# Pooled k by GpSimd sums and a DMA transpose, and tail u on array halves, in an attention and mixer kernel

## The chip, the cores and the metric

The kernel runs on one core of one Trainium2 chip. The metric is the device time of one execution in microseconds. The core has five engines with queues of their own, which run in order and meet through semaphores: PE (TensorE, matmuls), DVE (VectorE), ACT (ScalarE), POOL (GpSimd) and SP (SyncE, which here only issues DMAs). In this kernel PE writes to PSUM, DVE and ACT read PSUM and SBUF, and POOL works in SBUF and issues the loads, which also turn float32 into bf16. SP issues the output stores and the DMA transposes, which turn blocks of 128x128 bf16 in SBUF.

## What is computed

Batch 8, 8 heads, 576 rows, head size 64. First attention with pooled k and v (means over 8 rows, so 72 keys), then a mixer over rows ("token") and channels, with d_tok 256 and d_ch 1536:

```python
k_p = k.reshape(B, H, Sp, pool, D).mean(axis=3)      # pool = 8, Sp = 72
v_p = v.reshape(B, H, Sp, pool, D).mean(axis=3)
scores = scale * np.matmul(q, k_p.transpose(0, 1, 3, 2))
attn = softmax(scores)                                # over the 72 keys
x = heads_side_by_side(np.matmul(attn, v_p))          # (8, 576, 512)
h = np.maximum(x.transpose(0, 2, 1) @ w_tok1, 0.0) @ w_tok2
u = x + h.transpose(0, 2, 1)
out = u + np.maximum(u @ w_ch1, 0.0) @ w_ch2
```

## The kernel before, in words

**Tiles.** The 576 rows of a batch are 512 main rows and 64 tail rows. The main rows lie as 4 blocks of 128 rows (j = 0 to 3); the tail rows of two batches share one tile of 128 rows, one batch in partitions 0 to 63 and the other in 64 to 127. The pairs (`groups`) are (0, 7), (1, 2), (3, 4) and (5, 6); "slot" is a batch's place in its pair. PSUM tiles come from one ring of six (`pa`), so a PSUM tile that nobody has read yet can hold PE up.

**Stages of a batch.**
- *Pooled k*: `pool_k_sum` (L262) multiplies k by a pooling matrix, with k as the stationary operand: 32 matmuls for the main rows (L271) and 8 for the tail (L275), each with 64 output columns, on one half of the array or the other. The result lies transposed (head dimension in partitions) in two PSUM tiles. `pool_k_copy` (L279) casts it with two ACT and two DVE instructions (L284, L285) into `kbd`, a block-diagonal tile, two heads at a time. There are three `kbd` buffers.
- *Pooled v*: for batches 0 and 1 by matmuls (L292). From batch 2 on, v is loaded with 8 consecutive rows per partition (72 partitions, tile `vs`, two DMAs, L135), and `sum_v` (L296) adds the 8 rows on POOL, for two heads at a time, with three instructions (L302, L303, L304): twelve per batch. The sum goes to `vpx`.
- *Scores*: q is transposed on PE or by DMA (L553 for the main rows, L413 for tails). `Unit.do_S` makes the scores of half of the main rows on PE (L330), takes the maximum and subtracts it on DVE (L333, L335); `do_E` exponentiates on ACT (L343); `do_PT` transposes the probabilities, from batch 2 on with two DMAs on SP (L350). `TailUnit` does the same for tails, for both batches of a pair at once (L431, L437, L439, L446, L452); for pair (5, 6) it therefore needs `kbd` of 5 and of 6.
- *Values*: `values` (L394) multiplies probabilities and `vpx`; DVE divides by the sums (L398, L399). For tail pairs the two batches take the two halves of the array.
- *Token mix*: `do_AT` (L479, L483), then `do_u` (L513 for the blocks, L518 for a tail tile), each followed by a DVE addition of x (L515, L520). The tail's u is one accumulation of four matmuls with 128 output columns: the second matrix lies in two tiles `w2t`, padded with zeros, so that each batch adds to its own half of the rows. A tail's u is made with the pair's second batch, so after batches 2, 4, 6 and 7. `do_uT` transposes u by DMA on SP (L525).
- *Channel mix*: `channel_mix` makes GT (L776, ACT L778) and the output (L791, DVE L801), stored by SP (L829, L833). This is the bulk of PE's work.

**Order.** Each engine executes its instructions in the order in which the Python code emits them. For each batch b the channel mix of b is the main stream; the side stream holds the values and token mix of b + 1 (`value_stream`) and then the scores of b + 2 (`score_stream`). `weave` (L29) merges the two by costs written beside the items. The pooled k of batch b + 1 stands in the token mix of b (`mix_stream`, L580) if b + 1 opens a pair or belongs to the first two pairs; the pooled k of a pair's second batch stands in the score stream of the first (`own[1:]` in L701). Loads of batch b + 2 are issued by POOL in `load_gated` (L750): a tiny copy waits for the last transposed probabilities of batch b, then come the DMAs of k, q and v, then the twelve additions for v. Since POOL works in order, the next gate stands behind those additions.

Of the kernel before, what the change touches and what calls it, by code (L numbers as in the profile page):

```python
# [8 lines left out]
FP32 = mybir.dt.float32  # L9
BF16 = mybir.dt.bfloat16  # L10
# [38 lines left out]
def kernel(  # L49
# [56 lines left out]
    group_of = {b: g for g, members in enumerate(groups) for b in members}  # L106
    slot_of = {b: members.index(b) for members in groups for b in members}
    half = [slice(0, TAIL), slice(TAIL, P)]
    main_t, tail_t = {}, {}
    x_main, x_tail, u_main, uT_main, u_tail, uT_tail, ATs = {}, {}, {}, {}, {}, {}, {}  # L110

# [7 lines left out]
    def load(b, which=(0, 1, 2)):  # L119
        g = group_of[b]  # L120
        if b not in tail_t:
            tail_t[b] = [tail_pool.tile([P, H, D], BF16, name=n) for n in ("kt", "qt")]
            if b == 2:
                for t in tail_t[b]:
                    nc.gpsimd.memset(t[half[0]], 0.0)
            else:
                tail_t[groups[g][1]] = tail_t[b]
        main_t.setdefault(b, [None] * 3)
        for i in which:
            src = (k, q, v)[i]  # L130
            if i == 2 and b > 1:

                vs = v_pool.tile([P, H, POOL, D], BF16, name="vs")
                for r in (slice(0, SPM), slice(SPM, SP)):
                    nc.gpsimd.dma_start(out=vs[r].rearrange("p h t d -> p h (t d)"),  # L135
                                        in_=src[b].rearrange("h (p t) d -> p h (t d)", t=POOL)[r])
                main_t[b][i] = vs
                continue
            mt = (v_pool.tile([P, H, POOL, D], BF16, name="vs")[:, :, 0:NJ, :] if i == 2 else
                  kv_pool.tile([P, H, NJ, D], BF16, name=("km", "qm")[i]))  # L140
            main_t[b][i], tt = mt, tail_t[b][i]
            nc.gpsimd.dma_start(out=mt.rearrange("p h j d -> p h (j d)"),
                                in_=src[b, :, 0:MAIN, :].rearrange("h (p j) d -> p h (j d)", j=NJ))
# [52 lines left out]
    NB = 3  # L196
    kbd = [singles.tile([P, H, 2, SP], BF16, name=f"kbd{i}") for i in range(NB)]
    vpx = [singles.tile([SP, H, D + 1], BF16, name=f"vpx{i}") for i in range(NB)]
    for i in range(NB):
        eng = nc.vector if i == 0 else nc.any  # L200
        eng.memset(kbd[i], 0.0)
        eng.memset(vpx[i][:, :, D], float(POOL))

    NPB = 4
    prob_m = [singles.tile([P, 2, H, P], BF16, name=f"prob_m{i}") for i in range(NPB)]
    prob_t = [singles.tile([P, 2, HP, P], BF16, name=f"prob_t{i}") for i in range(2)]
# [14 lines left out]
    w1t = [singles.tile([P, DT], BF16, name=f"w1t{s}") for s in range(2)]  # L221
    w2r = gt_pool.tile([P, 2, S], BF16, name=f"GT{MAIN}")
    w2m = singles.tile([P, 2, NJ, P], BF16)
    w2t = [singles.tile([P, 2, P], BF16, name=f"w2t{s}") for s in range(2)]
    wc1 = singles.tile([P, 4, DC], BF16)
    wc2 = singles.tile([P, NM, DM], BF16)

    def load_w_tok():
        for s in range(2):
            nc.any.memset(w1t[s][half[1 - s]], 0.0)  # L230
            nc.any.memset(w2t[s][:, :, half[1 - s]], 0.0)
        nc.gpsimd.dma_start(out=w1m, in_=moe_w_tok1[0:MAIN, :].rearrange("(p j) n -> p j n", j=NJ))
        nc.gpsimd.dma_start(out=w1t[0][half[0], :], in_=moe_w_tok1[MAIN:S, :])
        nc.gpsimd.dma_start(out=w2r, in_=moe_w_tok2.rearrange("(c p) n -> p c n", p=P))
        nc.gpsimd.dma_start(out=w1t[1][half[1], :], in_=moe_w_tok1[MAIN:S, :])

    def split_w_tok2():
        for m in range(2):
            nc.gpsimd.tensor_copy(out=w2m[:, m], in_=w2r[:, m, 0:MAIN].rearrange("p (t j) -> p j t", j=NJ))
        for s in range(2):  # L240
            nc.gpsimd.tensor_copy(out=w2t[s][:, :, half[s]], in_=w2r[:, :, MAIN:S])

    def load_w_ch1():
        for i in range(3):
# [13 lines left out]

    def pool_k(b):
        pool_k_copy(b, pool_k_sum(b))  # L260

    def pool_k_sum(b):  # L262
        g, s = group_of[b], slot_of[b]
# [31 lines left out]

    def sum_v(b):  # L296

        vs, add = main_t[b][2][0:SP], ALU.add
        for h0 in range(0, H, 2):
            hs = slice(h0, h0 + 2)  # L300
            s4 = sum_pool.tile([P, 2, 4, D], FP32, name="s4")[0:SP]
            nc.gpsimd.tensor_tensor(out=s4, in0=vs[:, hs, 0:4], in1=vs[:, hs, 4:8], op=add)  # L302
            nc.gpsimd.tensor_tensor(out=s4[:, :, 0:2], in0=s4[:, :, 0:2], in1=s4[:, :, 2:4], op=add)  # L303
            nc.gpsimd.tensor_tensor(out=vpx[b % NB][:, hs, 0:D], in0=s4[:, :, 0], in1=s4[:, :, 1], op=add)  # L304

    class Unit:

# [31 lines left out]
        def do_E(self, i):  # L339
            h0, h1 = BANKS[i]  # L340
            if self.probs is None:
                self.probs = prob_m[(2 * self.b + self.jj) % NPB]
            nc.scalar.activation(out=self.probs[:, :, h0:h1, 0:SP].rearrange("p e h n -> p h e n"),  # L343
                                 in_=self.sh[i][:, 0:(h1 - h0) * 2].rearrange("p (h e) n -> p h e n", e=2),
                                 func=AF.Exp, scale=scale)

        def do_PT(self, e):
            self.pT[e] = pt_pool.tile([P, H, P], BF16, name="pT")
# [54 lines left out]
    class TailUnit:  # L403
# [39 lines left out]
        def do_E(self):  # L443
            self.probs = prob_t[self.g % 2]
            for i, sh in enumerate(self.sh):
                nc.scalar.activation(out=self.probs[:, i, :, 0:SP], in_=sh[:, 0:HP], func=AF.Exp, scale=scale)  # L446

        def do_PT(self):
            n = len(self.bs) * HP
# [16 lines left out]
    def token_mix(b):  # L466
# [40 lines left out]
                        acts(m, at_both[m])  # L507

        def do_u(j):
            u_ps = ps.tile([P, DM], FP32, name="pa")  # L510
            if j < NJ:
                for m in range(2):
                    nc.tensor.matmul(out=u_ps, lhsT=w2m[:, m, j, :], rhs=ATs[b][:, m, :],  # L513
                                     start=(m == 0), stop=(m == 1))
                nc.vector.tensor_tensor(out=u_main[b][:, j, :], in0=u_ps, in1=x_main[b][:, j, :], op=ALU.add)  # L515
            else:
                for i in range(4):
                    nc.tensor.matmul(out=u_ps, lhsT=w2t[i // 2][:, i % 2, :], rhs=ATs[groups[g][i // 2]][:, i % 2, :],  # L518
                                     start=(i == 0), stop=(i == 3))
                nc.vector.tensor_tensor(out=u_tail[g], in0=u_ps, in1=x_tail[g], op=ALU.add)  # L520

        def do_uT(j):
            us = u_main[b][:, j, :] if j < NJ else u_tail[g]
# [56 lines left out]
    def mix_stream(st, b, pooled=()):  # L580

        g, s = group_of[b], slot_of[b]
        add = adder(st)
        if b:
            u_main[b] = u_pool.tile([P, NJ, DM], BF16, name="um")
        uT_main[b] = u_pool.tile([P, 4, MAIN], BF16, name="uTm")
        if s == 1:
            u_tail[g] = ut_pool.tile([P, DM], BF16, name="ut")
            uT_tail[g] = ut_pool.tile([P, 4, P], BF16, name="uTt")
        do_AT, do_both_AT, do_u, do_uT, do_xT, do_uT0 = token_mix(b)  # L590
        if b == 0:
            return do_both_AT, do_xT, do_uT0
        add(1080, do_AT, 0)
        add(1080, do_AT, 1)
        for bb in pooled:
            add(KP, pool_k, bb)
        nj = NJ + s
        for j in range(nj + 1):
            if j < nj:
                add(690, do_u, j)  # L600
            if j >= 1:
                add(0, do_uT, j - 1)
# [98 lines left out]
    def score_stream(st, b):  # L701

        add = adder(st)
        a, c, t = parts[b]
        own = owned(b)
        if b == 3:
            add(KP, pool_k, b)
        add(SC, a.do_S, 0)
        add(SC, a.do_S, 1)
        add(0, a.do_E, 0)  # L710
        add(SC, a.do_S, 2)
        add(0, a.do_E, 1)
        add(0, a.do_E, 2)
        add(0, a.do_PT, 0)
        add(0, a.do_PT, 1)
        add(SC, c.do_S, 0)
        for bb in own[1:]:
            add(KP, pool_k, bb)
        add(SC, c.do_S, 1)
        add(0, c.do_E, 0)  # L720
        add(SC, c.do_S, 2)
        add(0, c.do_E, 1)
        add(0, c.do_E, 2)
        add(0, c.do_PT, 0)
        add(0, c.do_PT, 1)
        if t:
            add(2 * SC, t.do_S)
            add(0, t.do_E)
            add(0, t.do_PT)

    def value_stream(st, b):

# [17 lines left out]
    def load_gated(b, ready):  # L750

        nc.gpsimd.tensor_copy(out=gate, in_=ready())
        if b == 4:

            load(b - 1, (2,))
            load(b, (0, 2, 1))
            sum_v(b - 1)
        else:
            load(b, (0, 2, 1) if slot_of[b] else (0, 1, 2))
        sum_v(b)  # L760

    def channel_mix(uTs, us, dst, width, early=0):
# [90 lines left out]
               mybir.EngineType.SP, mybir.EngineType.Pool}  # L853
    with tc.manual_schedule(engines=engines):
        weave(Stream(), first_stream())
        for b in range(B):
            side = Stream()
            if b == 0:
                second_stream(side)
            elif b + 1 < B:  # L860
                value_stream(side, b + 1)
            if b + 2 < B:
                score_stream(side, b + 2)

            weave(c_stream(b), side, (2592.0, 3456.0)[b] if b <= 1 else 1728.0, 3456.0 if b == B - 2 else 1728.0)


# [28 lines left out]
```

## Time and profile before

| | us |
|---|---|
| runs: median of three (lowest, highest) | 282.71 (282.39, 283.29) |
| the profiled execution | 283.01 |
| its span, first to last instruction | 281.1 |
| PE busy | 270.1 |
| DVE, ACT, POOL busy | 161.1, 122.6, 104.4 |

The profile shows one execution. For each engine it counts the time in which instructions ran; matmuls overlap in the record, so a matmul's own duration (379 ns for 512 columns) is longer than its share of PE, and the distance from one start to the next is the better price. The granted TensorE clock is recorded as full (1.00) over the span, and the 16 DMA engines are busy at 90% or more in 20 consecutive of its 40 slices, from the second on. Times in the text are microseconds from the span's start. A row of the timeline gives start, duration, engine, line, operation, the tiles written and read, shape, and how many equal instructions were merged; in brackets stands idle time of the engine before it and what ended it. A row of the waits gives who waited for whom, the total, how often, and the longest.

### The profile page before, as it was taken

How to read it: one execution, taken by the hardware profiler on the slowest of the kernel's cores; microseconds unless marked ns; L12 is line 12 of the kernel's file. 1: busy time of each engine (PE TensorE's matmuls, PEld its weight loads, DVE VectorE, ACT ScalarE, POOL GpSimd, SP SyncE). 2: the span in 40 equal slices, each digit the busy share in tenths (PEclk: the TensorE clock that was granted, in tenths of full speed). 3: DMA queues.
4: the chain of work that ended last, by engine and by line, in shares of the span. 5: the costliest groups of instructions: out<-in, count | busy, mean ns of one | idle time of the engine just before them, and what ended most of it. 6: DMA issues, size and time to landing. Idle time of an engine off the chain costs nothing.

```text
span 281.1 us, 5671 instructions
## 1 busy us (share of the span) xinstructions
PE 270.1 (96%) x2221; PEld 146.2 (52%) x2258; DVE 161.1 (57%) x368; ACT 122.6 (44%) x223; POOL 104.4 (37%) x153
## 2 busy tenths in 40 slices
PE   6799999999999999999999999999999999999995
PEld 4575565565445444475545454475444444554463
DVE  4695297597559952784469753775369542520012
ACT  8582896336515453045533552054514550037220
POOL 8666543590639958058429161830000000000000
PEclk9999999999999999999999999999999999999999
DMA  7999999999999999999996899659135901341013
GB/s 81 181 204 199 193 206 196 197 168 224 171 161 180 181 229 148 197 223 174 169 186 143 182 204 190 138 150 209 28 75 128 190 20 40 94 112 40 37 40 113
DMA packets 99963, 42.16 MB, mean 150 GB/s; under 512 B 69728, under 2 KB 95328, under 8 KB 99936
## 3 DMA queue, kind: packets, MB, share of 16 engines
q0 software_dynamic: 36016, 17.93, 49.2%
q1 hardware_dynamic: 63776, 23.74, 42.0%
q8 instruction: 18, 0.29, 0.4%
q10 hardware_dynamic: 144, 0.13, 0.1%
q14 instruction: 9, 0.07, 0.1%
HBM read 35.85 MB, written 9.44 MB: 161 GB/s over the span
## 4 chain that ended last, share of the span: by engine, by line
PE 84%; DMA 9%; POOL 4%; issue 1%; DVE 0%; ACT 0%; POOLq 0%
PE pa L791 33%; PE pa L776 30%; PE pa L513 4%; PE pa L479 4%; DMA qm<-in_q_dram 4%; DMA GT<-in_moe_w_tok_dram 3%; PE pa L394 3%; PE pa L330 3%; DMA pT<-prob_t 2%; PE pa L271 1%; PE pa L518 1%; PE pa L483 1%; PE pt L319 1%; POOL qm L152 1%; PE pt L357 1%
## 5 line engine op out<-in xcount | busy, mean ns | idle before, releaser
L791 PE MATMUL pa<-wc,GT 128*128 128x512 bf16 (+1 forms) x427 | 102.3, 373 | 0.9 <-issue 0.2
L778 ACT ACTIVATE GT<-pa 128x512 bf16<-128x512 f32 x105 | 62.3, 597 | 64.6 <-PE pa L776 59.5
L776 PE MATMUL pa<-uTm,wc 128*128 128x512 bf16 x356 | 88.6, 379 | 0.7
L776 PEld LDWEIGHTS <-wc 128*128 128x128 bf16 x564 | 44.9, 98 | 35.9 <-issue 0.3
L791 PEld LDWEIGHTS <-GT 128*128 128x128 bf16 x444 | 41.5, 98 | 40.7
L343 ACT ACTIVATE prob_m<-sh 128x432 bf16<-128x432 f32 (+1 forms) x48 | 24.5, 521 | 50.5 <-DVE sh L335 30.6
L302 POOL TENSOR_TENSOR s<-vs 72x512 f32<-72x512 bf16 x24 | 27.6, 1149 | 35.4 <-DMA vs<-in_v_dram 33.9
L801 DVE TENSOR_TENSOR o<-pa,um 128x512 f32<-128x512 f32 (+1 forms) x29 | 19.3, 669 | 25.3 <-PE pa L791 24.2
L335 DVE TENSOR_TENSOR sh<-pa,mx 128x432 f32<-128x432 f32 (+1 forms) x48 | 26.8, 558 | 5.1 <-ACT GT L778 0.5
L333 DVE TENSOR_REDUCE mx<-pa 128x6 f32<-128x432 f32 (+1 forms) x48 | 26.4, 550 | 3.4 <-PE pa L330 3.3
L399 DVE TENSOR_TENSOR xm<-pa,den 128x256 bf16<-128x256 f32 x56 | 23.8, 425 | 1.9
L398 DVE RECIPROCAL den<-pa 128x4 f32<-128x4 f32 (+1 forms) x66 | 11.7, 177 | 20.9 <-PE pa L394 20.7
L515 DVE TENSOR_TENSOR um<-pa,xm 128x512 bf16<-128x512 f32 x28 | 18.8, 688 | 8.1 <-PE pa L513 7.9
L475 DVE TENSOR_SCALAR AT<-pa 128x512 bf16<-128x512 f32 x8 | 5.5, 692 | 22.3 <-PE pa L483 20.8
L303 POOL TENSOR_TENSOR s<-s 72x256 f32<-72x256 f32 x24 | 17.4, 723 | 1.9
L394 PEld LDWEIGHTS <-pT 72*128 72x128 bf16 (+1 forms) x280 | 12.3, 100 | 9.7 <-issue 1.3
L330 PE MATMUL pa<-kbd,qT 128*128 128x144 bf16 x128 | 15.4, 226 | 0.5 <-ACT qT L321 0.5
L513 PE MATMUL pa<-AT,w2m 128*128 128x512 bf16 x56 | 15.8, 379 | 0.1
L330 PEld LDWEIGHTS <-qT 128*128 128x128 bf16 x128 | 10.6, 98 | 8.8 <-ACT qT L321 1.4
L394 PE MATMUL pa<-vpx,pT 72*128 72x65 bf16 (+1 forms) x280 | 14.1, 194 | 1.0 <-ACT pT L457 0.5
L479 PE MATMUL pa<-xm,w1m 128*128 128x512 bf16 x56 | 14.4, 379 | 0.1
L776 PE MATMUL pa<-uTt,wc 128*128 128x128 bf16 x192 | 11.9, 219 | 0.0
(126 smaller groups left out, 240.5 us busy)
## 6 DMA issues: line engine op xcount, KB each, us to landing
out_dram<-o SPq DMA_DIRECT2D x31, 256.0 KB, 2.8
km<-in_k_dram POOLq DMA_DIRECT2D x8, 512.0 KB, 8.5
vs<-in_v_dram POOLq DMA_DIRECT2D x8, 512.0 KB, 10.9
qm<-in_q_dram POOLq DMA_DIRECT2D x7, 512.0 KB, 12.2
wc<-in_moe_w_ch_dram POOLq DMA_DIRECT2D x6, 512.0 KB, 12.3
out_dram<-o SPq DMA_DIRECT2D x9, 128.0 KB, 2.5
kt<-in_k_dram POOLq DMA_DIRECT2D x8, 64.0 KB, 7.5
qm<-in_q_dram POOLq DMA_DIRECT2D x2, 256.0 KB, 5.1
```

Of the source, the lines that this page charges most:

```text
L302: nc.gpsimd.tensor_tensor(out=s4, in0=vs[:, hs, 0:4], in1=vs[:, hs, 4:8], op=add)
L330: nc.tensor.matmul(out=sc[:, (h - h0) * 2:(h - h0) * 2 + 2, :], lhsT=qTs[self.b][:, 2 * h + self.jj, :], rhs=kbd[self.b % NB][:, h], start ...
L333: nc.vector.tensor_reduce(out=mx[:, 0:n], in_=sc, axis=AX.X, op=ALU.max)
L335: nc.vector.tensor_tensor(out=sh[:, 0:n], in0=sc, in1=mx[:, 0:n, None].broadcast_to([P, n, SP]), op=ALU.subtract)
L343: nc.scalar.activation(out=self.probs[:, :, h0:h1, 0:SP].rearrange("p e h n -> p h e n"), in_=self.sh[i][:, 0:(h1 - h0) * 2].rearrange("p ...
L394: nc.tensor.matmul(out=ao[r, hh, :], lhsT=probs_of(h, r), rhs=vpx[b % NB][:, h, :], start=True, stop=True)
L399: nc.vector.tensor_tensor(out=xo[rows, hf * HP * D:(hf + 1) * HP * D].rearrange("p (h d) -> p h d", d=D), in0=ao[rows, :, 0:D], in1=den[ro ...
L479: nc.tensor.matmul(out=at_ps, lhsT=w1m[:, j, m * P:(m + 1) * P], rhs=x_main[b][:, j, :], start=(j == 0), stop=False)
L513: nc.tensor.matmul(out=u_ps, lhsT=w2m[:, m, j, :], rhs=ATs[b][:, m, :], start=(m == 0), stop=(m == 1))
L776: nc.tensor.matmul(out=g_ps[:, i, :], lhsT=wc1[:, kk, m * P:(m + 1) * P], rhs=uTs[:, kk, :], start=(kk == 0), stop=(kk == 3))
L778: nc.scalar.activation(out=GT[:, m0:m0 + per, :], in_=g_ps, func=AF.Relu)
L791: nc.tensor.matmul(out=hold["ps"], lhsT=GT[:, kk, j * P:(j + 1) * P], rhs=wc2[:, kk, cols], start=(kk == 0), stop=(kk == NM - 1 and us is ...
```

## The change

It has two parts.

*k of batches 5, 6 and 7* is loaded like v, with 8 rows per partition in 72 partitions (from the same two buffers as v), and summed on POOL by the same twelve instructions, before those for v. The sums go to `ksum`, which is batch 0's old k tail tile. One DMA transpose on SP (`ksum_T`) turns them into `ksT`, batch 0's old v tail tile, and four DVE copies (`ksum_copy`) bring them into `kbd`. The mean's division by 8 moves into the scale of the exponential. The pooling matmuls, their four casts, and the loads of these three batches' k tails go. There is one `ksum` and one `ksT`. For 5 and 7 the transpose stands in the score stream of 4 and of 6, ahead of the probabilities' transposes of the first half, and the copies where the pooled k stood. For 6 the transpose stands in the score stream of 5 after the last scores, and the copies two items later; the scores, exponentials and transposes of tail pair (5, 6) move to the main stream of the following batch, behind its first item.

*u of a pair's tails*: `w2t` becomes one unpadded tile of 64 columns. For each m the two batches' matmuls follow each other, each with 64 output columns on its own half of the array and in a PSUM tile of its own; two DVE additions over 64 partitions replace one over 128.

In the built program PE has 40 matmuls less for each of the three batches, POOL 12 additions more, SP one transpose more; the order of the other instructions shifts a little where the merge counts costs differently. In batch 3's main stream the four casts go, and the tail scores of (5, 6) stand behind the first four L776 of batch 4's; there the last u block and the tail's u come four L791 later than before.

```diff
+    KSUM = (5, 6, 7)
...
-            if i == 2 and b > 1:
+            if i == 2 and b > 1 or i == 0 and b in KSUM:
...
+    ksum = tail_t[0][0]
+    ksT = tail_t[0][2].rearrange("p h d -> p (h d)").rearrange("p (r n) -> p r n", n=P)
...
-    w2t = [singles.tile([P, 2, P], BF16, name=f"w2t{s}") for s in range(2)]
+    w2t = singles.tile([P, 2, TAIL], BF16)
...
-        for s in range(2):
-            nc.gpsimd.tensor_copy(out=w2t[s][:, :, half[s]], in_=w2r[:, :, MAIN:S])
+        nc.gpsimd.tensor_copy(out=w2t, in_=w2r[:, :, MAIN:S])
...
+    def ksum_T(b):
+        nc.sync.dma_start_transpose(out=ksT, in_=ksum.rearrange("p h d -> p (h d)"))
+
+    def ksum_copy(b):
+        heads = kbd[b % NB].rearrange("p (r t) e n -> p r t e n", t=2)
+        for hl in range(2):
+            src = ksT[hl * D:(hl + 1) * D, :, 0:SP]
+            nc.vector.tensor_copy(out=heads[0:D, :, hl, 0, :], in_=src)
+            nc.vector.tensor_copy(out=heads[D:P, :, hl, 1, :], in_=src)
...
+    def scale_of(b):
+
+        return scale / POOL if b in KSUM else scale
...
-            else:
-                for i in range(4):
-                    nc.tensor.matmul(out=u_ps, lhsT=w2t[i // 2][:, i % 2, :], rhs=ATs[groups[g][i // 2]][:, i % 2, :],
-                                     start=(i == 0), stop=(i == 3))
-                nc.vector.tensor_tensor(out=u_tail[g], in0=u_ps, in1=x_tail[g], op=ALU.add)
+            u_ps = [ps.tile([P, DM], FP32, name="pa") for _ in range(2)]
+            for m in range(2):
+                for i, bb in enumerate(groups[g]):
+                    nc.tensor.matmul(out=u_ps[i][half[i]], lhsT=w2t[:, m, :], rhs=ATs[bb][:, m, :],
+                                     start=(m == 0), stop=(m == 1))
+            for i in range(2):
+                nc.vector.tensor_tensor(out=u_tail[g][half[i]], in0=u_ps[i][half[i]], in1=x_tail[g][half[i]], op=ALU.add)
...
         for bb in pooled:
-            add(KP, pool_k, bb)
+            if bb in KSUM:
+                add(0, ksum_copy, bb)
+            else:
+                add(KP, pool_k, bb)
...
+        for bb in owned(b + 1)[:1] if b + 1 < B else []:
+            if bb in KSUM:
+                add(0, ksum_T, bb)
         add(0, a.do_PT, 0)
...
+        late = [bb for bb in own[1:] if bb in KSUM]
         for bb in own[1:]:
-            add(KP, pool_k, bb)
+            if bb not in KSUM:
+                add(KP, pool_k, bb)
...
         add(SC, c.do_S, 2)
+        for bb in late:
+            add(0, ksum_T, bb)
         add(0, c.do_E, 1)
         add(0, c.do_E, 2)
         add(0, c.do_PT, 0)
+        for bb in late:
+            add(0, ksum_copy, bb)
         add(0, c.do_PT, 1)
+        if t and late:
+            return [(0, t.do_S), (0, t.do_E), (0, t.do_PT)]
...
+        if b in KSUM:
+            sums_of(main_t[b][0][0:SP], ksum[0:SP])
         sum_v(b)
...
+            side, main = Stream(), c_stream(b)
+
+            main.items[1:1] = last
+            last = []
...
             if b + 2 < B:
-                score_stream(side, b + 2)
+                last = score_stream(side, b + 2)
```

`sums_of` is the body of the old `sum_v` with the destination as an argument.

More of the change, by code (lines that the diff above doesn't have):

```diff
@@ L230, in load_w_tok @@
             nc.any.memset(w1t[s][half[1 - s]], 0.0)
-            nc.any.memset(w2t[s][:, :, half[1 - s]], 0.0)
         nc.gpsimd.dma_start(out=w1m, in_=moe_w_tok1[0:MAIN, :].rearrange("(p j) n -> p j n", j=NJ))
@@ L296, in sum_v, with sums_of @@
     def sum_v(b):
-        vs, add = main_t[b][2][0:SP], ALU.add
+        sums_of(main_t[b][2][0:SP], vpx[b % NB][:, :, 0:D])
+    def sums_of(vs, dst):
+        add = ALU.add
         for h0 in range(0, H, 2):
@@ L303, in sum_v @@
             nc.gpsimd.tensor_tensor(out=s4[:, :, 0:2], in0=s4[:, :, 0:2], in1=s4[:, :, 2:4], op=add)
-            nc.gpsimd.tensor_tensor(out=vpx[b % NB][:, hs, 0:D], in0=s4[:, :, 0], in1=s4[:, :, 1], op=add)
+            nc.gpsimd.tensor_tensor(out=dst[:, hs], in0=s4[:, :, 0], in1=s4[:, :, 1], op=add)
+    def scale_of(b):
+        return scale / POOL if b in KSUM else scale
     class Unit:
@@ L344, in do_E @@
                                  in_=self.sh[i][:, 0:(h1 - h0) * 2].rearrange("p (h e) n -> p h e n", e=2),
-                                 func=AF.Exp, scale=scale)
+                                 func=AF.Exp, scale=scale_of(self.b))
         def do_PT(self, e):
@@ L445, in do_E @@
             for i, sh in enumerate(self.sh):
-                nc.scalar.activation(out=self.probs[:, i, :, 0:SP], in_=sh[:, 0:HP], func=AF.Exp, scale=scale)
+                nc.scalar.activation(out=self.probs[:, i, :, 0:SP], in_=sh[:, 0:HP], func=AF.Exp,
+                                     scale=scale_of(self.bs[0]))
         def do_PT(self):
@@ L509, in do_u @@
         def do_u(j):
-            u_ps = ps.tile([P, DM], FP32, name="pa")
             if j < NJ:
+                u_ps = ps.tile([P, DM], FP32, name="pa")
                 for m in range(2):
@@ L515, in do_u @@
                 nc.vector.tensor_tensor(out=u_main[b][:, j, :], in0=u_ps, in1=x_main[b][:, j, :], op=ALU.add)
-            else:
-                for i in range(4):
-                    nc.tensor.matmul(out=u_ps, lhsT=w2t[i // 2][:, i % 2, :], rhs=ATs[groups[g][i // 2]][:, i % 2, :],
-                                     start=(i == 0), stop=(i == 3))
-                nc.vector.tensor_tensor(out=u_tail[g], in0=u_ps, in1=x_tail[g], op=ALU.add)
+                return
+            u_ps = [ps.tile([P, DM], FP32, name="pa") for _ in range(2)]
[5 more added lines that the diff above has]
+                nc.vector.tensor_tensor(out=u_tail[g][half[i]], in0=u_ps[i][half[i]], in1=x_tail[g][half[i]], op=ALU.add)
         def do_uT(j):
@@ L729, in score_stream @@
             add(0, t.do_PT)
+        return []
     def value_stream(st, b):
@@ L855 @@
         weave(Stream(), first_stream())
+        last = []
         for b in range(B):
-            side = Stream()
+            side, main = Stream(), c_stream(b)
+            main.items[1:1] = last
+            last = []
             if b == 0:
@@ L862 @@
             if b + 2 < B:
-                score_stream(side, b + 2)
-            weave(c_stream(b), side, (2592.0, 3456.0)[b] if b <= 1 else 1728.0, 3456.0 if b == B - 2 else 1728.0)
+                last = score_stream(side, b + 2)
+            weave(main, side, (2592.0, 3456.0)[b] if b <= 1 else 1728.0, 3456.0 if b == B - 2 else 1728.0)
 _INS = ['q', 'k', 'v', 'moe_w_tok1', 'moe_w_tok2', 'moe_w_ch1', 'moe_w_ch2']
```

## The prediction

> **What bounds the kernel.** I read the page's first part, then the waits of PE, then PE's timeline around the lines that the change touches.
>
> ```profile
> PE 270.1 (96%) x2221; PEld 146.2 (52%) x2258; DVE 161.1 (57%) x368; ACT 122.6 (44%) x223; POOL 104.4 (37%) x153
> ```
>
> PE is busy 96% of the span. Its waits say whether that is PE's own work (columns: us in total, times, longest):
>
> ```profile
> PE pa L292 <- DMA vs<-in_v_dram: 0.9, 1, 0.9
> ...
> PE pa L394 <- ACT pT L457: 0.5, 1, 0.5
> PE pa L330 <- ACT qT L321: 0.5, 2, 0.3
> PE pa L394 <- DMA pT<-prob_t: 0.5, 1, 0.5
> ```
>
> The largest wait, 2.2 us for DVE, is the start. After 106 us no wait of PE is over 0.1 us. So PE time taken out in the middle is worth its full length, and every new wait of PE costs its full length: nothing downstream gives it back.
>
> Durations of matmuls overlap, so I price PE work from start to start. Start, duration, instruction:
>
> ```profile
> 138.56 1.03 PE L776 MATMUL pa<-uTm,wc 128*128 128x512 bf16 x4
> 139.52 0.69 PE L271 MATMUL pa<-pool_m,km 128*64 128x64 bf16 x32
> 140.05 0.27 PE L275 MATMUL pa<-pool_t,kt 128*64 128x8 bf16 x8
> 140.25 1.04 PE L776 MATMUL pa<-uTm,wc 128*128 128x512 bf16 x3
> ```
>
> Four 512-column matmuls take 0.86 us (0.216 each, as L513 x4 from 142.42 to 143.28). Those from 138.56 would be followed at 139.43; L271 starts at 139.52 and the next L776 at 140.25. One pool_k therefore holds PE for 0.82 us, of which 0.09 is the change to half-width matmuls.
>
> **The sum, part by part.**
>
> *pool_k of 5, 6 and 7 leaves PE*: 3 x 0.82 = 2.47 us less. The other two (150.54, 201.47) stand in the same gap of 0.82 us.
>
> *u of the tails*: four full-width matmuls, 0.86 us, become two pairs on halves. Whether the halves run side by side is seen at the values of a tail pair:
>
> ```profile
> 167.25 0.59 PE L776 MATMUL pa<-uTm,wc 128*128 128x512 bf16 x2
> 167.77 0.45 PE L394 MATMUL pa<-vpx,pT 72*64 72x65 bf16 x16
> 168.15 0.39 PE L776 MATMUL pa<-uTm,wc 128*128 128x512 bf16 x1
> ```
>
> Sixteen 65-column matmuls on halves, with two different moving operands, take 0.38 us: 24 ns each, where the stream alone is 65/512 x 216 = 27 ns. So they overlap. I take two pairs of 0.216, 0.09 to enter the half mode (as at L271) and 0.11 to leave it (0.38 minus eight pairs at 33 ns, the pace of L271's sixteen pairs in 0.53 us): 0.63 us, 0.23 us saved, four times 0.9. Bounds: 1.7 saved if the two mode changes are free, 0.8 lost if the halves do not overlap at 512 columns. The second VectorE add (64x512 takes 683 ns, L386, hardly less than 128x512) is off PE's path.
>
> PE's own work thus falls by **3.4 us**.
>
> *The sums on GpSimd*: twelve more adds per batch; one set of twelve took 10.2 us (122.22 to 132.41). k of 5 is issued first, at 106.3, and lands 6.2 us later as km does now, or up to 11 as v does; I take 6.7 (64 KB more), so its sums end at 123.4. Those of v end at 133.7, 1.3 later than now, and the next gate and loads move by as much: k of 6 issued at 134.6, landed after 8.1 (km) to 10.8 (v), summed by 153.0 to 155.7. Nobody waits for v's sums before 159.
>
> *The transpose on SP's queue*: one more issue of 1.2 us (uTm, 28 of them) ahead of the pT transposes of batches 4 and 6. Batch 4: pT issued at 124.04 lands 4.4 later, at 128.4; the values (L394) start at 130.18, and 0.23 us earlier after the change. With 1.25 us more, 129.7 against 129.95: just hidden. I put 0.2 us, 0 to 1.5. Batch 6: the slack is 2.1 us (185.99 + 4.0 against 192.13); nothing.
>
> *Batch 6's kbd is the place that decides.* Its copies now feed the tail scores of 5 and 6 (L431), moved behind the first four L776 of the next batch. *When PE gets there*: those L776 start at 158.00 now. Ahead of them two pool_k (1.64), two u tails (0.46) and L431 itself (0.33) are gone: 155.6, plus 0.86 for the four: **156.4**. *When the transpose is issued*: in the new order it stands on SP behind batch 5's first pT pair and an output store, and these hang on VectorE's queue. The u tail ends at 145.9 on PE (145.44, minus 1.05 saved, plus 0.86 because four L791 more stand ahead, plus 0.63). From 146.1 VectorE does two ut adds and an output add (0.60 each from start to start), three score pairs (1.23, 1.23, 0.92) and an output add (0.60): 151.9. On SP then:
>
> ```profile
> 151.68 3.06 SPq L350 DMA_TRANSPOSE pT<-prob_m  x2
> 154.83 0.53 SPq L829 DMA_DIRECT2D out_dram<-o  x1
> ```
>
> A store (0.4), two pT (3.1) and a store (0.6): the transpose goes out at 156.1. k's sums are there by then. Transposes of this size (uTt) land after 2.4 to 8.7, median 2.5: **158.6**. VectorE is free from 155.9 and waits.
>
> *The copies* are the one operation of which the trace has almost no row: VectorE from SBUF to SBUF. Only L183 does that, two identical copies of 64x8, while GpSimd issues DMAs:
>
> ```profile
> L183 DVE COPY pool_t<-diag x2: 162/322/481, 4.5 to 4.6; 64x8 bf16<-64x8 bf16 x2
> ```
> ```profile
> 4.45 0.68 DVE L183 COPY pool_t<-diag 64x8 bf16<-64x8 bf16 x2 [0.38 <-POOL diag L178]
> ```
> ```profile
> 4.36 1.55 POOL L152 DMA_DIRECT2D qm<-in_q_dram  x2
> ```
>
> One took 162 ns and its twin 481: something of GpSimd's held it. Alone, four copies of 288 elements cost 4 x 0.16 plus the elements (at most 0.14 each, from 425 and 677 ns for 512 and 1024 bf16 elements from PSUM): 0.7 to 1.2 us, say 0.9. But at 158.6 GpSimd sums v of 6, end to end, for 10 us:
>
> ```profile
> 153.01 1.15 POOL L302 TENSOR_TENSOR s<-vs 72x512 f32<-72x512 bf16 x1
> 154.24 0.72 POOL L303 TENSOR_TENSOR s<-s 72x256 f32<-72x256 f32 x1
> 155.03 0.46 POOL L304 TENSOR_TENSOR vpx<-s 72x128 bf16<-72x128 f32 x1
> ```
>
> If each copy is held by the add that is running, the first waits some 0.4 and the other three one add each, together a round of 2.5 us: 3.8 us in all. Lower bound 0.7 (no hold), upper 1.2 + 4 x 1.15 = 5.8. I take 3.8, since the twin of L183 was held directly after the first one got through.
>
> The Trainium skill, page "SBUF — State Buffer", section "Who interferes with whom", says that VectorE in a two-port mode, which copies between SBUF tiles enter, and GpSimd exclude each other from a shared port pair for a whole instruction. By it the copies cost the 3.8 us; without it 0.9, and the kernel would come out about as before. The trace agrees as far as two copies can; no add beside a copy is in it.
>
> PE then starts L431 at 158.6 + 3.8 + 0.1 = 162.5 instead of 156.4: a **wait of 6.1 us**. Queued behind it on PE are the next GT blocks and batch 5's values, and everything after those. The pT of the tails follows at about 169 (2.0 of VectorE, 0.5 of ScalarE, 3.4 for the transpose) and is needed 9 us after L431 starts, at 171: no second wait. Copies of 5 and 7 fall at 140 and about 203, when GpSimd waits for loads or is done: nothing. The casts that leave ScalarE and VectorE save nothing on PE's path.
>
> Sum on the profiled execution, 283.01 us (its span of 281.1 and 1.9 around it): 283.01 - 3.4 + 0.2 + 6.1 = 285.9. That execution is 0.3 over the median of the runs, 282.71, so **285.6**.
>
> **Rivals.**
> 1. *The port is free*: copies cost 0.9, PE waits 3.2. 283.01 - 3.4 + 0.2 + 3.2 - 0.3 = **282.7**, as before. For it: the first L183 copy was not held. Decides at: copies under 1.5 us.
> 2. *The transposed sum is there in time* (not slower): then 283.01 - 3.4 - 0.3 = **279.3**, to 281.3 with 2 us of waiting left. It decides if the data has landed by 155.4, that is, with the transpose issued 3 us sooner than my chain through VectorE and SP says. Against it: that chain has no idle time from 146.1 to 156.1; for it: each link is only inferred from today's spacing.
> 3. *The long wait also lets PE's clock fall.* At the start 22 matmuls of 288 columns (L257) take 5.46 us, 240 ns from one to the next, twice the 121 that 216 ns per 512 give. A cold stretch as long as that loses 2.7 us: **288.3**. Later waits of 0.9 us or less left the granted clock at 1.00.
> 4. *The halves do not overlap at 512 columns*: 1.7 us more than in any of these; within the range.
>
> The Trainium skill, page "TensorE: Matmul & The Clock Gate", Part 1, says that an idle window of about 3.4 us halves the clock. By it the third rival follows from a 6 us wait and not from the first rival's 3.2; no run here shows a wait that long.
>
> **How the numbers follow.** Forecast 0.40, port free 0.22, in time 0.22, clock 0.16. About 0.3% (0.85 us) is what a measurement of this kernel can tell from no change. Faster: the second rival and 0.03 of the first, 0.25. Same: 0.15 of the first. Slower: the rest, 0.60. For the range I leave out half of the second rival below and half of the third above: 280.0 to 287.6; the forecast alone, by the bounds of the copies and of batch 4's wait, has 282.5 to 288.6, and its middle is 284 to 287.
>
> **What would show it.** PE's waits: one line L451 (L431 now) released by VectorE's kbd copies, 6 us (3 by rival 1, none by rival 2). The copies: about 1 us each for batch 6, about 0.2 for 5 and 7. The SP timeline: ksT issued near 156 and after two pT. PE: 0.63 us for each u tail, and no matmuls of pool_k after 90 us. A PEclk under 9 near 160 us would be rival 3. I am wrong if the copies of 6 end before 159.

## The result and the profile after

The changed kernel takes 286.64 us (median of 6 runs, 286.25 to 289.51), the kernel before 282.55 (6 runs, 282.19 to 283.29): ratio 1.0152, 95% interval 1.0123 to 1.0181. It is slower by 4.1 us; the forecast was 285.6 in a range of 280.0 to 287.6. A few runs below were slower as a whole (over 1.5% above the fastest of their kernel) and are left out of the ratios, not of the medians, so where the two differ the ratio counts.

The profiled execution took 286.82 us. Page of the changed kernel, first part and slices:

```profile
span 285.1 us, 5479 instructions
...
PE 267.8 (94%) x2103; PEld 143.5 (50%) x2138; DVE 166.3 (58%) x377; ACT 120.0 (42%) x216; POOL 131.0 (46%) x188
...
PE   6699999999999999999998399999999999999994
...
PEclk9999999999999999999999689999999999999999
```

PE has 118 instructions fewer and 2.3 us less busy time, yet the span is 4.0 us longer. The row of PE has one hole, in the 22nd and 23rd slices (8 and 3; 150 to 164 us), and the row of the clock a dip in the 23rd and 24th (6 and 8; 157 to 171 us). The waits of PE name the place (us in total, times, longest):

```profile
PE pa L451 <- DVE kbd L272: 3.0, 1, 3.0
PE pa L451 <- DVE kbd L273: 2.3, 1, 2.3
```

L451 are the tail scores of batches 5 and 6; L272 and L273 are the copies of batch 6's transposed sums. After 100 us no other wait of PE is over 0.2 us. Timeline of PE there (start, duration, instruction, idle time before it):

```profile
158.96 0.26 PE L451 MATMUL pa<-kbd,qTt 64*64 64x72 bf16 x2 [3.03 <-DVE kbd L272]
161.51 0.40 PE L451 MATMUL pa<-kbd,qTt 64*64 64x72 bf16 x13 [2.30 <-DVE kbd L273]
```

PE is ready at 158.96 - 3.03 = 155.93 and starts the bulk at 161.51: 5.3 us idle in two pieces, since the first copy releases a few matmuls (0.25 us) and the rest wait for the last copy. The sums of k had been done since 152.47, but on SP the transpose stood behind batch 5's first pT pair and an output store, and went out at 155.16:

```profile
152.02 0.45 POOL L320 TENSOR_TENSOR kt<-s 72x128 bf16<-72x128 f32 x1
```
```profile
151.78 2.67 SPq L370 DMA_TRANSPOSE pT<-prob_m  x2
154.54 0.53 SPq L871 DMA_DIRECT2D out_dram<-o  x1
155.16 1.22 SPq L266 DMA_TRANSPOSE vt<-kt  x1
```

(`kt` and `vt` are the old tiles in which the sums and the transposed sums lie.) The copies on VectorE, and the adds of GpSimd beside them (v of batch 6):

```profile
157.82 1.08 DVE L272 COPY kbd<-vt 64x288 bf16<-64x288 bf16 x1 [2.53 <-DMA vt<-kt]
158.94 0.77 DVE L273 COPY kbd<-vt 64x288 bf16<-64x288 bf16 x1
159.72 0.52 DVE L272 COPY kbd<-vt 64x288 bf16<-64x288 bf16 x1
160.25 1.22 DVE L273 COPY kbd<-vt 64x288 bf16<-64x288 bf16 x1
```
```profile
157.67 1.15 POOL L318 TENSOR_TENSOR s<-vs 72x512 f32<-72x512 bf16 x1
158.90 0.72 POOL L319 TENSOR_TENSOR s<-s 72x256 f32<-72x256 f32 x1
159.69 0.45 POOL L320 TENSOR_TENSOR vpx<-s 72x128 bf16<-72x128 f32 x1
160.22 1.15 POOL L318 TENSOR_TENSOR s<-vs 72x512 f32<-72x512 bf16 x1
```

Add start and duration in both fences: the adds end at 158.82, 159.62, 160.14 and 161.37, the copies at 158.90, 159.71, 160.24 and 161.47, each 0.1 us behind one add. The same copy for batch 5, while GpSimd runs no add:

```profile
139.23 0.22 DVE L272 COPY kbd<-vt 64x288 bf16<-64x288 bf16 x1
```

So 0.22 us became 0.5 to 1.2, and the four take 3.65 us instead of 0.9. The stretches before, in and after the dip of the clock (window, length, busy time of PE, PEld, DVE, ACT and POOL, granted clock, DMA share, GB/s):

```profile
150.00:158.90 8.90, 5.88 (x33) 2.80 (x33) 5.96 (x11) 3.00 (x6) 8.12 (x11) 1.00 0.83 185
158.90:165.83 6.93, 4.35 (x31) 2.12 (x32) 5.86 (x13) 1.37 (x3) 3.48 (x5) 0.51 0.34 83
165.83:172.00 6.17, 6.12 (x50) 3.17 (x49) 3.24 (x12) 3.66 (x7) 3.14 (x6) 1.00 0.91 140
```

The clock is halved for 6.8 us, and PE is busy for 4.35 of the second window. Work takes twice as long there: four L818 matmuls go from 161.85 to 163.53, 1.68 us instead of 0.86. Half of 4.35, 2.2 us, is thus what the slow clock costs.

**Where the time went.** I compare the start of one output add of VectorE in both traces. Just before this place (128.65 in before) the changed kernel is 1.01 us ahead; at the add that stands at 174.84 in before it is 4.91 behind. This stretch, which I use for all experiments below, is thus 5.92 us longer. It lost two pool_k (1.64) and one u of the tails (0.20, as the kernel with that alone shows): PE has 1.84 less to do, so 7.76 have to be explained. 5.33 are the wait; 2.4 are left, and 2.2 of them are the slow clock. On PE the changed kernel is then 3.87 behind at batch 7's tail scores (215.39 in before, 219.26), since batch 7's pool_k and the u of pair (5, 6) are gone, 1.04 together, and 3.75 behind at the end.

### The profile page after: what moved, and what is told of

It reads as the page before. It is cut to its first block, busy times and chain, and to the rows that moved or that the text cites. A ratio compares the mean times of both kernels' runs of the same rounds, so it can differ in the third digit from the quotient of the medians.

```text
span 285.1 us, 5479 instructions
## 1 busy us (share of the span) xinstructions
PE 267.8 (94%) x2103; PEld 143.5 (50%) x2138; DVE 166.3 (58%) x377; ACT 120.0 (42%) x216; POOL 131.0 (46%) x188
## 4 chain that ended last, share of the span: by engine, by line
PE 81%; DMA 7%; POOL 6%; DVE 2%; issue 2%; ACT 1%; POOLq 0%
PE pa L818 29%; PE pa L833 29%; PE pa L534 4%; PE pa L500 4%; DMA vs<-in_k_dram 3%; PE pa L414 3%; PE pa L350 2%; POOL s L318 2%; DMA qm<-in_q_dram 2%; POOL s L319 1%; DMA pT<-prob_m 1%; PE pa L855 1%; DMA vt<-kt 1%; PE pa L504 1%; PE pt L377 1%
## 5 line engine op out<-in xcount | busy, mean ns | idle before, releaser
L818 PE MATMUL pa<-uTm,wc 128*128 128x512 bf16 x357 | 89.8, 384 | 0.9 <-issue 0.2
L818 PEld LDWEIGHTS <-wc 128*128 128x128 bf16 x564 | 45.3, 98 | 37.6 <-issue 2.2
L318 POOL TENSOR_TENSOR s<-vs 72x512 f32<-72x512 bf16 x36 | 41.4, 1149 | 22.8 <-DMA vs<-in_k_dram 12.0
L319 POOL TENSOR_TENSOR s<-s 72x256 f32<-72x256 f32 x36 | 26.0, 722 | 2.8
L818 PE MATMUL pa<-uTt,wc 128*128 128x128 bf16 x192 | 11.9, 219 | 0.0
```

Source lines behind the costliest of these rows:

```text
L818: nc.tensor.matmul(out=g_ps[:, i, :], lhsT=wc1[:, kk, m * P:(m + 1) * P], rhs=uTs[:, kk, :], start=(kk == 0), stop=(kk == 3))
```

## The experiments

Stretch is the difference to before of that stretch. Rest is the stretch plus what PE lost there (1.84; 1.64 without the new u; 0.20 where k of 5 and 6 stays on PE), minus the wait at the tail scores and minus filler matmuls at 0.216 us. Cold is the time at half clock in that profile. Half of PE's busy time in it is 1.6 to 1.7 us where cold is 3.4, and 2.2 to 2.9 where it is 6.8; what of the rest remains beyond that, 0.2 to 0.4 us, and the 0.3 to 0.7 of the kernels without a fall, stays open. "At 282.55" is the ratio times before's median.

```
kernel                     ratio [95%]             at 282.55  stretch  wait  rest  cold
changed kernel             1.0152 [1.0123 1.0181]   286.8      5.92    5.33  2.4   6.8
u of the tails alone       0.9987 [0.9960 1.0013]   282.2     -0.20    0     0     0
v sums of 6 left out       1.0050 [1.0024 1.0077]   284.0      3.04    2.85  2.0   3.4
14 filler matmuls          1.0104 [1.0058 1.0150]   285.5      3.35    1.47  0.7   0
copies as reductions       1.0114 [1.0055 1.0173]   285.8      4.87    3.48  3.2   6.8
k of 7 only                0.9947 [0.9908 0.9987]   281.1     -0.20    0     0     0
26 filler matmuls          1.0122 [1.0080 1.0164]   286.0      4.04    0     0.3   0
earlier and not held       0.9953 [0.9921 0.9985]   281.2     -0.68    0.59  0.6   0
also later                 0.9969 [0.9937 1.0002]   281.7      1.94    1.77  2.0   3.4
earlier only               1.0071 [1.0033 1.0108]   284.6      3.21    3.01  2.0   3.4
not held only              1.0102 [1.0049 1.0156]   285.4      4.51    3.50  2.9   6.8
k alone                    1.0177 [1.0115 1.0240]   287.6      6.15    4.78  3.0   6.8
```

On the chips of these runs most kernels scatter by 2 to 5 us (before itself: 281.9 to 286.2), which the intervals show; the mechanisms are read from the stretches of the profiles.

My theory: the change saves PE time everywhere and loses it at one place, by a transpose late on SP, copies held by GpSimd's adds, and a clock that falls in the wait.

**The u of the tails alone** (`KSUM = (5, 6, 7)` becomes `KSUM = ()`).

> Only u of the tails on the halves; k of all batches stays on PE's matmuls. My theory: four matmuls side by side in two pairs take 0.63 us instead of 0.86, four times, so PE's work falls by 0.9 us and nothing new is waited for: 281.6 us against 282.55, ratio 0.997. Rival (the halves do not overlap at 512 columns): about 1 us slower than before, 283.4. Rival (the second VectorE addition delays somebody): 282.5 or more, with PE waits that before does not have.

282.86 us, ratio 0.9987. The halves overlap: in the changed kernel the four matmuls hold PE from 144.56 to 145.11 and the mode change, 0.64 us instead of 0.86, and the stretch, which has one of them, is 0.20 shorter. In the whole time the gain isn't told from no change (the interval holds both the expected 0.997 and 1). This profile has a wait of 0.8 us at 98 us for a pT transpose, which before lacks. It isn't slower by 1 us.

**GpSimd idle beside the copies** (the sums of batch 6's v are left out).

```diff
-        sum_v(b)
+        if b != 6:
+            sum_v(b)
```

> The whole change, with the twelve GpSimd additions for v of batch 6 left out (its values are made from what the buffer held), so GpSimd is idle when VectorE copies the transposed k of batch 6. My theory (GpSimd's additions hold VectorE's copies): each copy takes 0.23 us as for batches 5 and 7, the four 0.94 instead of 3.64; PE's wait for them falls from 5.3 to 2.6 us; the clock does not fall; 286.6 - 2.7 - 2.4 = 281.5 us. Rival (the copies are slow because the transposed data arrives piece by piece, or because of load on the DMA side): the copies stay at 3.6 us and the time at 286.6.

VectorE's timeline:

```profile
158.04 0.23 DVE L272 COPY kbd<-vt 64x288 bf16<-64x288 bf16 x1 [2.68 <-DMA vt<-kt]
```

All four take 0.23: the hold is GpSimd's, as theory said. PE waits 2.3 + 0.5 us, as expected. But the time is 284.35 (284.0 by the ratio) and not 281.5. The clock fell all the same, for 3.4 us in the profile, and nine of the ten runs have the mean clock of this profile (0.993 or 0.994). My expectation that a wait under 3 us leaves the clock alone was wrong. The fall costs 1.6 us, half of the 3.2 that PE was busy in it; the tenth run, with a mean clock of 0.999, is the fastest, but at 283.37 it isn't at 281.5 either: what the rest of the difference is stays open.

**Filler matmuls ahead of the tail scores**: 14, later 26, whose results nobody reads.

```diff
-            return [(0, t.do_S), (0, t.do_E), (0, t.do_PT)]
+            return [(0, lambda: warm(14)), (0, t.do_S), (0, t.do_E), (0, t.do_PT)]
```

> The whole change, with 14 matmuls of 512 columns on an idle tile put on PE ahead of the tail scores of batches 5 and 6 (3.0 us of work in a wait of 5.3). My theory (the long wait lets PE's clock fall to half for 6.8 us, which costs some 2.4 us): the tail scores start at the same time, 161.5, PE's wait is 2.3 us, the granted clock stays at 1.00, and the time falls to 284.2 us. Rival (what is lost after the wait is not the clock but late data behind it): 286.6, whatever the clock does. Rival (the added work costs as much as it saves): 286.6 or more.

> As the changed kernel, with 26 filler matmuls of 512 columns (5.6 us) ahead of the tail scores, so that PE has work through the whole wait of 5.3 us. Theory (the long idle stretch lets the clock fall, 2.6 us on top of the wait): PE idle under 0.5 us there, granted clock 0.998 or more in every run, 284.0 us. Rival (the clock falls for another reason, or the 2.6 us are not the clock's): 286.6 as the changed kernel, with the clock at 0.5 for several microseconds all the same.

Windows, first with 14, then with 26 (the clock is the third number from the end):

```profile
156.00:162.00 6.00, 4.48 (x42) 2.17 (x42) 4.27 (x8) 0.42 (x2) 5.45 (x8) 1.00 0.66 136
```
```profile
156.00:166.50 10.50, 10.45 (x68) 4.81 (x68) 7.11 (x13) 2.17 (x4) 9.56 (x13) 1.00 1.08 214
```

In both profiles the clock stays at 1.00 and the rest falls from 2.4 to 0.7 and 0.3; with 26 the bulk of the tail scores starts as late as in the changed kernel, 5.7 us after PE has come to them (165.24 against 159.54) where it was 5.8 (161.51 against 155.71). So the fall comes from PE's idleness, and without it this place is 1.7 to 2.1 us cheaper. With 14 the copies end about 1 us sooner than in the changed kernel, mostly since the first one met the end of an add (last section); so 0.8 of the gain of that profile, 284.35 where 284.2 was expected, is a shorter wait, and the agreement is partly luck. In two of the four runs with 14 the mean clock is 0.994, as after a fall of 3.4 us: 14 don't keep it up every time. The medians don't show the gain: 286.09 and 286.77. With 26 the clock is 1.00 in all six runs, but they take 285.19 to 289.02; the profiled one, 289.02, lost 3.4 us against before between output adds at 97 and 113 us: PE waited 1.2 us for VectorE at 88, 1.7 for a uTm transpose and 0.9 for a pT transpose, where before waited 0.5. Why those transposes are late in some executions stays open: waits for them of 0.8 us and more at that place stand in five of the experiments' profiles, whatever their edit. The interval (284.8 to 287.2 at 282.55) excludes my 284.0; 5.6 us of filler is also 0.3 more than the wait.

**Reductions over one element instead of copies** (the same movement of data by another instruction).

```diff
-            nc.vector.tensor_copy(out=heads[0:D, :, hl, 0, :], in_=src)
-            nc.vector.tensor_copy(out=heads[D:P, :, hl, 1, :], in_=src)
+            for out in (heads[0:D, :, hl, 0, :], heads[D:P, :, hl, 1, :]):
+                nc.vector.tensor_reduce(out=out[:, :, :, None], in_=src[:, :, :, None], axis=AX.X, op=ALU.max)
```

> The whole change, with the four VectorE copies of each batch written as a maximum over an axis of length one: the same engine, the same place, the same data, another instruction. If it is the form of the copy that GpSimd's additions hold (a shared way into SBUF that a plain copy takes and a reduction does not), each takes about 0.45 us, as a reduction of 288 elements does, for batches 5, 6 and 7 alike: 1.8 to 2.2 us for batch 6 instead of 3.64, PE's wait 3.9 instead of 5.3. Rival (any VectorE instruction that reads and writes SBUF is held): 0.5 to 1.2 us each for batch 6, and the wait 5.3 or more.

VectorE's timeline:

```profile
159.11 1.85 DVE L273 TENSOR_REDUCE kbd<-vt 64x288 bf16<-64x288 bf16 x4 [2.44 <-DMA vt<-kt]
```

0.46 us each, end to end, while GpSimd's adds run: not held. The transpose is issued 1.4 us later in this execution (156.53), PE waits 3.5 us, and the clock is at half for 6.8.

**k of batch 7 only** (`KSUM = (7,)`).

> Only batch 7's k is summed on GpSimd and transposed; k of 5 and 6 goes through PE as before, the tail scores of 5 and 6 stand where they stood before, and the u of the tails is on halves. My theory: all the loss of the change sits at batch 6's copies, so this is faster: 282.45 - 0.82 (one pool_k less) - 0.9 (four u tails at 0.23) = 280.7 us, or 281.2 if the u tails bring only the 0.4 that the kernel with them alone showed; no wait of PE of a microsecond or more, granted clock 1.00 to the end. Rival, the longer work on GpSimd's and SP's queues costs wherever it is put (later loads and gates, later pT): 282.3 or more, with a wait for a DMA on PE after 160 us.

280.83 us, ratio 0.9947: faster than before. No wait of PE over 0.1 us after 100 us, and the stretch is 0.20 shorter, the u alone. Behind it PE is 1.13 ahead of before, and at batch 7's tail scores 2.17: 1.04 for batch 7's pool_k and one u, where 0.82 + 0.23 were expected. The sums, the transpose and the copies cost PE nothing where they have time.

**The two halves of the wait, apart and together.** Earlier:

```diff
         add(0, a.do_PT, 0)
+        for bb in late:
+            add(0, ksum_T, bb)
         add(0, a.do_PT, 1)
...
         add(SC, c.do_S, 2)
-        for bb in late:
-            add(0, ksum_T, bb)
```

> As the changed kernel, with batch 6's transpose between batch 5's first two pT transposes, and nothing else: the four copies stay plain ones on VectorE. Theory (the wait has two parts, the place on SP and the held copies): it is issued when the sums are there (152.5 to 155.3 in the runs so far), lands 2.5 us later, the copies are held for 3.6 us and end near 160; PE waits 3 to 4 us in two pieces, the clock falls for at least one stretch of 3.4 us: 284 to 285 us, wait 1.3 to 2.3 us less than in the changed kernel. Rival (the place alone is the fault): copies in 1 us, a wait under 1 us, 280 to 281 us.

The transpose goes out at 154.39 and lands at 156.8, 1.0 sooner; the copies take 3.5 us (0.94, 0.77, 0.52, 1.22, the round of adds again), and PE waits 0.7 + 2.3 us. The place alone is not the fault.

Not held: batch 6's four copies by `nc.scalar.copy`.

> As the changed kernel, with batch 6's four copies on ScalarE; the transpose stays where the change puts it. Theory: it lands near 157.8, four copies of 0.44 take 1.8 us while GpSimd's adds run, PE waits 2.0 + 1.6 = 3.6 us, the clock falls for 3.4 or 6.8 us: 284 to 286 us. Rival (the held copies alone are the fault): a wait under 2 us and the clock at 1.00, 281 us. Rival (ScalarE is held by GpSimd as VectorE is): copies of 0.5 to 1.2 each as on VectorE, 286.6 us.

ScalarE's timeline:

```profile
160.55 0.43 ACT L273 COPY kbd<-vt 64x288 bf16<-64x288 bf16 x1 [2.11 <-DMA vt<-kt]
```

0.43 each beside GpSimd's adds: ScalarE is not held. PE waits 3.5 us, the clock falls. The hold alone is not the fault either. Together: earlier, `hl == 0` by ScalarE's copy and `hl == 1` by VectorE's reduction.

> As the changed kernel, with batch 6's transpose issued between batch 5's first two pT transposes instead of behind an output store after them, two of a batch's four copies on ScalarE and two as reductions on VectorE. Theory (the wait is the transpose's place on SP plus the held copies): the transpose goes out near 153.1 when the sums are there (152.5), lands at 155.7, ScalarE (2 x 0.39 from 155.8) and VectorE (2 x 0.45) end at 156.6, PE reaches the tail scores at 155.9 and waits 0.7 us; clock 1.00; 282.45 - 3.2 + 0.7 = 280.0 us. Rival (the second pT, now 1.3 us later, is late for the values; or ScalarE's copies are held as well): a wait of 1 to 3 us at the values or at L451, 281 to 283 us.

Waits of PE at this place, and SP's timeline:

```profile
PE pa L454 <- ACT kbd L274: 0.3, 1, 0.3
PE pa L454 <- DVE kbd L276: 0.3, 1, 0.3
```
```profile
152.66 1.29 SPq L373 DMA_TRANSPOSE pT<-prob_m  x1
154.21 1.19 SPq L266 DMA_TRANSPOSE vt<-kt  x1
```

0.6 us of wait where 0.7 was expected, the second pT in time, the clock at 1.00 there: 281.47 us, ratio 0.9953, faster than before. Only the fastest of twelve runs come near the expected 280.0 (280.29, 280.40); in one of the twelve the mean clock is 0.994, as after a fall of 3.4 us. SP stands free from 153.95 to 154.21: now the sums of k (done at 154.18 here, at 152.47 in the changed kernel) end last.

**Also later**: the tail scores behind eight L818 instead of four.

```diff
-            main.items[1:1] = last
+            main.items[2:2] = last
```

The gate of batch 7's loads goes behind batch 5's first values.

> As the kernel before it in this list, with the tail scores one block of four matmuls later (behind eight instead of four L818) and the gate of batch 7's loads behind batch 5's first values. Theory: PE reaches the tail scores at 156.8, when the copies (156.6) are done: no wait; the tails' pT lands 7.2 us later, at 164, before the tail values; 282.45 - 3.2 = 279.2 us. Rival: the wait only moves on, to the tail values or to the loads of batch 7 (their gate comes 1 to 2 us later): 280.0 us or more.

No better: the time is the rival's, 281.7 by the ratio, but not for its reason: the wait stays at the tail scores and has other causes. Waits of PE:

```profile
PE pa L454 <- DVE o L849: 1.0, 1, 1.0
PE pa L454 <- ACT kbd L274: 0.7, 1, 0.7
```

Batch 6's k was loaded later in this execution and its sums ended at 155.3, so the transpose still decides (0.7); and the scores' second PSUM tile now waits for an output add that stands behind the two reductions on VectorE (1.0). 1.8 us of idleness brought the clock down for 3.4 us in this execution. The other eleven runs, with mean clocks of 0.997 and more, show no such fall.

**k alone**, with u of the tails on the full width as before.

> The first part of the change without the second: k of 5, 6 and 7 summed on GpSimd, u of the tails by four full-width matmuls as before. Theory: the same long wait and the same fall of the clock, and four u tails at 0.23 us more: 287.2 to 287.5 us. Rival (the halves' u brings nothing): 286.6 us as the changed kernel.

Ratio 1.0177, 287.6 at 282.55, with waits of 2.5 and 2.3 us and the same 6.8 us of half clock. The expected 287.2 to 287.5 lies in the interval, as 286.8 does: the runs don't settle the sign of the u's share, the stretch (0.20) does.

## Why the prediction was right, point by point

- *pool_k, 0.82 us each*: right. Where batch 7's and the u of pair (5, 6) were, PE gains 1.04 both in the changed kernel (4.91 to 3.87 behind) and in the kernel with k of 7 only (1.13 to 2.17 ahead), as 0.82 + 0.23 says.
- *u of the tails, 0.23 each*: right; 0.20 in the stretch. The fourth rival (halves that do not overlap) is out. PE's timeline of the changed kernel:

```profile
144.56 0.62 PE L542 MATMUL pa<-AT,w2t 128*64 128x512 bf16 x4
145.11 1.04 PE L833 MATMUL pa<-wc,GT 128*128 128x512 bf16 x4
```

- *Batch 4's pT behind one more issue, 0.2 us*: wrong, but small; no wait came. Before's wait of 0.5 us for prob_t at 105.82, an earlier stage, is gone as well, in the changed kernel and in every experiment's profile; why stays open.
- *Sums of k of 6 done at 153.0 to 155.7*: 152.47 in the changed kernel, 154.18 and 155.3 in two of the experiments, by when k was loaded.
- *PE reaches the tail scores at 156.4*: 155.93. *Transpose issued at 156.1, landed at 158.6*: 155.16 and 157.80. The chain through VectorE and SP was right, a microsecond too long.
- *Copies held by one add each, 3.8 us*: 3.65. This was the disputed step, taken from one pair of 64x8 copies, and four kernels bear it out: without adds 0.23, on ScalarE 0.43, as reductions 0.46, earlier but beside adds 0.94, 0.77, 0.52, 1.22. The Trainium skill, page "SBUF — State Buffer", section "Who interferes with whom", says the same of all three: copies can take the port pair shared with GpSimd, reductions on trn2 cannot, and ScalarE waits for nobody.
- *Wait of 6.1*: 5.3. The transpose landed 0.8 sooner and the copies took 0.15 less, PE was ready 0.5 sooner, and 0.25 us of tail scores ran between the two pieces.
- *No second wait at the tail values*: right; pT of the tails landed at 168.75, the values start at 172.68.
- *The clock*: here the forecast missed a term. I made its fall a rival of 0.16, at 2.7 us, when the forecast's own wait of 6.1 was far over the 0.9 that I had seen leave it alone; it fell in every run of the changed kernel (mean clock 0.987 or 0.988 in all six), at a cost of 2.2 us by PE's busy time, where rival 3 had 2.7. Forecast and rival 3 were one case. The total, 285.6 against 286.64, came out close by luck, because the wait was 0.8 better and two smaller waits, 0.2 forecast and 0.5 in before, were missing, against 2.4 that the sum lacks: 285.9 - 0.8 - 0.7 + 2.4 = 286.8, the profiled execution. The step that failed is the sum's missing term, not its mechanism.
- *Rival 1 (port free)* is out by the copies, and its price of 282.7 was too low as well: with GpSimd idle the copies are free, and the time is 284.0, a fall of the clock included; *rival 2 (in time)* by the landing at 157.80, but the kernel with both cures shows what it would have given, 281.2. I put its price at 279.3; of the 1.9 between, 0.6 are the wait that is left and 0.6 the unexplained rest of that stretch; where the others are isn't shown.

## What to carry to other kernels

When PE is the bound, moving its work to another engine pays only as far as the result's whole way back (sums, transpose in a shared queue, copies, next reader) has slack at each batch: the same edit gained at batch 7 and lost at batch 6. Don't put plain SBUF-to-SBUF copies of VectorE on a critical path beside a busy GpSimd; ScalarE or a form that isn't held costs 0.43 to 0.46 instead of up to 1.2 us. And price a wait of PE with the clock's share on top: in the kernels whose profiles have 2.8 us of waiting and more and no filler, the clock fell in 39 of 40 runs, and in the profiles the fall cost 1.6 to 2.9 us.

## What the runs showed of the hardware that was not expected

- The clock falls after less idleness than I believed: in the kernel whose profile has waits of 2.3 + 0.5 us in 9 of 10 runs, and once after 0.75 + 1.02 us within 2 us. It stayed at 1.00 in the profiles with 0.6 us, and with 1.5 us after filler. The Trainium skill, page "TensorE: Matmul & The Clock Gate", Part 1, says that the clock halves after at least one idle window of about 3.4 us, and that these windows run freely; as a condition that PE be idle for 3.4 us the runs contradict it. The length agrees (next point), and the half clock lasts 3.4 or 6.8 us in every profile with a fall, one or two such windows, and costs half of PE's busy time in it, 1.6 to 2.9 us.
- The traces show how much idleness it takes here. In each profile the recorded changes of the clock lie whole steps of 3.41 us apart: in the changed kernel it rises at 5.41, falls at 159.00 and rises at 165.83, 45 and 2 steps. I laid all 13 profiles out in these steps, from the first rise on. Every step in which PE was idle for 2.1 us or more ends in half clock, and none with 1.71 or less ends a stretch of full clock; between them stand two, one that fell (1.82, in the kernel "also later") and one that did not (1.97, at the end of the kernel with 14 filler matmuls). So it takes about half a step. Half clock lasted a second step where PE was idle for 0.8 us or more in the first one (2.3 in the changed kernel). The steps start at another moment in each execution, so the same wait can lie in one of them or be split by two; that would explain why some kernels fall in some of their runs only, but the runs that weren't profiled can't show it.
- A held copy does not wait for GpSimd to run out of work: copies and adds alternate, and each copy ends 0.1 to 0.2 us after an add. GpSimd's adds keep their 1.15, 0.72 and 0.45 us. So the price depends on where in an add a copy comes: in both kernels with filler the first copy came just before an add's end and took 0.23 us, and the four took 2.7 us instead of 3.65.
